# Linear attention feeding a PReLU MLP on one core: norm steps moved ahead of the evacuations, two PSUM banks for the output tiles, and tokens on partitions from batch 2 instead of batch 3

## The chip, the cores and the metric

The kernel runs on one core of one Trainium2 chip. The metric is the device time of that core in microseconds. An execution's time is a little longer than its span, which runs from the first to the last instruction of the trace.

## The reference

Eight batches of eight heads, 576 tokens and 64 features each go through attention without a softmax, a root-mean-square norm, and a two-layer MLP:

```python
# attention, per batch and head: q, k, v are 576 x 64
kv = einsum('bhsd,bhse->bhde', k, v)          # 64 x 64
out = einsum('bhsd,bhde->bhse', q, kv)
rms = sqrt(mean(out * out, axis=-1) + 1e-06)
x = (out / rms * g_norm)                       # -> 4608 tokens x 512
# MLP: 512 -> 2048 -> 512
h = x @ w_in
g = maximum(h, 0) + alpha * minimum(h, 0)
y = g @ w_out
```

Inputs and output are float32; the kernel multiplies in fp16 and accumulates in float32.

## The kernel before

**Tiling.** The 4608 tokens are cut into nine windows of 512 (`NW`, `W`), which do not coincide with the batches of 576. In a window the first layer makes 16 groups (`NF`) of 128 features: four matmuls of 512 columns into an `h_ps` bank (L422), then an evacuation on two engines: ScalarE writes `relu(-h)` to `m_sb` (L429) and VectorE writes `gt = beta * m_sb + h` (L431). The second layer makes four output tiles of 128 tokens by 512, each a sum of 16 matmuls (L444), copied out of PSUM by ScalarE (`y_sb`, L451) and stored by two transfers issued from SyncE (L459).

**Interleaving.** A unit (L530) is one group of the first layer for window w and four matmuls of the second layer for window w-1. In a steady window 16 units follow one another. PSUM has three banks for `h_ps`, one for `y_ps` (tag `y`), one shared bank (tag `s`) and three banks for attention (`o0`, `o1`, `o2`).

**Attention, first form** (windows below `NB_PE` = 3). For each pair of heads j: five transposes of q on TensorE (`step_t`, L207) and a copy by VectorE; the product k'v for all heads of a batch (`step_kv`, L222) and a masking multiply on VectorE; q times kv into `ot_ps` (`step_ot`), squared by ScalarE; a matmul with a block mask that sums the squares (`ssq_mm`, L270), then Ln and Exp on ScalarE; and the multiply `xt` on VectorE (`norm`, L281). The tail (L293 to L317) does the same for those tokens of the last such batch that reach into the next window: 192 tokens here, in two pieces.

**Attention, second form** (batches 3 to 7, "tokens on partitions"). q of a batch is transposed by one DMA (`transpose_q`, L328). For each tile of 128 tokens, four short matmuls write `otm_ps` and ScalarE squares it (`tile_a`, L336); VectorE reduces (`tile_b`, L349); ScalarE takes Ln and Exp of the small result, and GpSimd spreads the factor times g over the row, `rg` (`tile_c`, L357); VectorE multiplies, `xrow`, and SyncE issues DMA transposes into `xm`, the next window's input (`tile_d`, L370). `phase_steps(w)` (L383) lists these steps so that a tile's a, b and c, d fall in three successive units: b runs in the middle of a unit, behind the evacuation in VectorE's order; c, a and d at its end.

**Order.** Every engine's instructions run in the order written here; SyncE and GpSimd each have their own. GpSimd issues the loads of k, q, v and of the weights (casting to fp16), copies k and q of batches 2 to 7 into another layout (`regroup`, L105), and does `rg`. There are two sets of buffers for q, k and v, so batch b+2 overwrites batch b.

**Start.** Batch 0 arrives in halves and is handled in the first form; single matmuls on constants (`keep_warm`, L193) fill some gaps. Then come the 16 groups of window 0, the second layer of window 0 for three of its four tiles with window 1's attention between (L521), window 1's first layer with the fourth tile and window 2's attention between (L543), and from window 2 on the steady units (L561). At the end stands the second layer of window 8 alone.

Of the kernel before, what the change touches and what calls it, by code (L numbers as in the profile page):

```python
# [9 lines left out]
FP32 = mybir.dt.float32  # L10
# [7 lines left out]
def kernel(  # L18
# [11 lines left out]
    nc = tc.nc  # L30
# [15 lines left out]
    NC = D_MODEL // P  # L46
    assert NC == NPAIR and 0 < REM < P
    inv_d = 1.0 / D
    NB_PE = 3

    const_p = ctx.enter_context(tc.tile_pool(name="constp", bufs=1))
    w_p = ctx.enter_context(tc.tile_pool(name="weights", bufs=1))
# [56 lines left out]
        )  # L109

    def load_batch(b):
        for nm in ("k", "q", "v"):
            load(b, nm)

    def regroup_batch(b):
        for nm in ("k", "q"):
            regroup(b, nm, eng=nc.gpsimd)

    for nm in "qkv":
# [12 lines left out]
    nc.vector.memset(mask32[64:128, 64:128], 1.0)  # L132
    mask16 = const_p.tile([P, P], FP16, name="mask16")
    nc.vector.tensor_copy(out=mask16[:], in_=mask32[:])
    warm16 = const_p.tile([P, W], FP16, name="warm16")
    nc.vector.memset(warm16[:], 0.5)
    eps_t = const_p.tile([P, 1], FP32, name="eps_t")
# [8 lines left out]
    nc.sync.dma_start(out=g2col[64:128, :], in_=g_norm[:].unsqueeze(1))  # L146
    alpha_row = const_p.tile([NF, P], FP32, name="alpha_row")
    nc.sync.dma_start(out=alpha_row[:], in_=moe_alpha[:].rearrange("(g p) -> g p", p=P))
    g_all = const_p.tile([P, D], FP32, name="g_all")
    nc.sync.dma_start(out=g_all[:], in_=g_norm[:].partition_broadcast(P))  # L150


    WQ = 4
# [36 lines left out]
        load_w_out(i)  # L190


    def keep_warm(n):  # L193
        ps = ps_s.tile([P, W], FP32, name="warm_ps", tag="s")
# [71 lines left out]
    def step_ssq(w, j):  # L266
        ssq_mm(w, j)
        norm(w, j)

    def ssq_mm(w, j):  # L270
        ot_ps, sq = ots.pop((w, j))
        ssq_ps = ps_o.tile([P, W], FP32, name="ssq_ps", tag="o2")
        nc.tensor.matmul(out=ssq_ps[:], lhsT=mask16[:], rhs=sq[:], start=True, stop=True)  # L273
        rstd = attn_p.tile([P, W], FP32, name="rstd")
        nc.scalar.activation(  # L275
            out=rstd[:], in_=ssq_ps[:], func=AF.Ln, bias=eps_t[:], scale=inv_d,
        )
        nc.scalar.activation(out=rstd[:], in_=rstd[:], func=AF.Exp, bias=0.0, scale=-0.5)  # L278
        ots[w, j] = (ot_ps, rstd)

    def norm(w, j):  # L281
        ot_ps, rstd = ots.pop((w, j))
        xts[w, j] = xt_p.tile([P, W], FP16, name="xt", tag=f"xt{j}")
        nc.vector.scalar_tensor_tensor(  # L284
            out=xts[w, j][:], in0=ot_ps[:], scalar=g2col[:], in1=rstd[:],
            op0=ALU.mult, op1=ALU.mult,
        )
# [48 lines left out]
    def tile_a(b, t):  # L336
        ot_ps = ps_o.tile([P, H, D], FP32, name="otm_ps", tag=f"o{n_tile[0] % 3}")
        n_tile[0] += 1
        for j in range(NPAIR):
            nc.tensor.matmul(  # L340
                out=ot_ps[:, 2 * j : 2 * j + 2, :], lhsT=qtms[b][:, t * NPAIR + j, :],
                rhs=kvs[b, j], start=True, stop=True,
            )
        n = P if t < TPP else REM
        sq = attn_p.tile([P, H, D], FP32, name="sqm_sb", tag="rstd")
        nc.scalar.activation(out=sq[0:n], in_=ot_ps[0:n], func=AF.Square)  # L346
        tiles[b, t] = [n, ot_ps, sq]

    def tile_b(b, t):  # L349
        n, _, sq = tiles[b, t]  # L350
        ss = attn_p.tile([P, H], FP32, name="ss", bufs=3)
        nc.vector.tensor_reduce(  # L352
            out=ss[0:n], in_=sq[0:n], op=ALU.add, axis=mybir.AxisListType.X,
        )
        tiles[b, t][2] = ss

    def tile_c(b, t):  # L357
        n, _, ss = tiles[b, t]
        nc.scalar.activation(  # L359
            out=ss[0:n], in_=ss[0:n], func=AF.Ln, bias=eps_t[0:n], scale=inv_d,  # L360
        )
        nc.scalar.activation(out=ss[0:n], in_=ss[0:n], func=AF.Exp, bias=0.0, scale=-0.5)  # L362
        rg = attn_p.tile([P, H, D], FP32, name="rg")
        nc.gpsimd.tensor_tensor(  # L364
            out=rg[0:n], in0=ss[0:n].unsqueeze(2).to_broadcast([n, H, D]),
            in1=g_all[0:n].unsqueeze(1).to_broadcast([n, H, D]), op=ALU.mult,
        )
        tiles[b, t][2] = rg

    def tile_d(b, t):  # L370
        n, ot_ps, rg = tiles.pop((b, t))
        x = attn_p.tile([P, H, D], FP16, name="xrow", bufs=3)
        nc.vector.tensor_mul(out=x[0:n], in0=ot_ps[0:n], in1=rg[0:n])  # L373
        i = 0
        while i < n:
            w, c = divmod(b * S + t * P + i, W)
            m = min(n - i, W - c)
            nc.sync.dma_start_transpose(
                out=xm(w)[:, :, c : c + m], in_=x[i : i + m].rearrange("p h d -> p (h d)"),
            )  # L380
            i += m

    def phase_steps(w):  # L383


        if w >= NW:
            return []
        todo = [(b, t) for b in range(NB_PE, min(B, w + 1)) for t in range(NT)
                if (b, t) not in done and b * S + t * P < (w + 1) * W]
        done.update(todo)  # L390
        steps = []
        if w == NB_PE:
            n = NPAIR // JT
            for i in range(n + 1):
                m = [lambda i=i: step_tail_ot(i)] if i < n else []
                m += [lambda i=i: step_tail_ssq(i - 1)] if i > 0 else []
                steps.append(([], m))
        for i in range(len(todo) + 2):
            a, b, d = ([todo[i - k]] if 0 <= i - k < len(todo) else [] for k in range(3))
            mid = [lambda x=x: tile_b(*x) for x in b]  # L400
            end = [lambda x=x: tile_c(*x) for x in b] + [lambda x=x: tile_a(*x) for x in a]
            end += [lambda x=x: tile_d(*x) for x in d]
            steps.append((mid, end))
        if w < B:
            steps[0][0].append(lambda: step_kv(w))
        return steps

    done = set()
# [40 lines left out]
    def y_out(y, w, a):  # L449
        y_sb = ysb_p.tile([P, D_MODEL], FP32, name="y_sb")  # L450
        nc.scalar.copy(out=y_sb[:], in_=y[:])  # L451
        for i in range(0, P, REM):
# [5 lines left out]
                rows = out[b * S + LONG : (b + 1) * S, :].rearrange("(p t) m -> t p m", t=TPP)  # L458
            nc.sync.dma_start(out=rows[t], in_=y_sb[i : i + REM, :])  # L459


    H_POOL = (ps_h, "h")
    keep_warm(10)
# [1 line left out]
    step_t(0, 0, H_POOL)  # L465
    step_t(0, 1, H_POOL)
    regroup(0, "k", 0, HH)
    keep_warm(3)
    step_kv(0, 0, 2)
    step_ot(0, 0)  # L470
    step_ot(0, 1)
    regroup(0, "q", HH, H)
# [11 lines left out]
    )  # L484
    regroup(0, "k", HH, H)
    ssq_mm(0, 0)
    ssq_mm(0, 1)
    step_kv(0, 2, 4)
    norm(0, 0)
    norm(0, 1)  # L490
    step_ot(0, 2)
    step_ot(0, 3, (ps_y, "y"))
    load_batch(2)
    first = [ps_h.tile([P, W], FP32, name="h_ps", tag="h") for g in range(3)]
    for g in range(3):
        m1_mm(first[g], 0, g, (0, 1))
    step_ssq(0, 2)
    keep_warm(2)
    step_ssq(0, 3)
    for g in range(3):  # L500
        m1_mm(first[g], 0, g, (2,))
    for g in range(3):
        m1_mm(first[g], 0, g, (3,))
        m1_evac(first[g], 0, g)
    for g in range(3, NF):
        m1_group(0, g)
        if g == 10:
            regroup(1, "k")
        if g == 14:
            regroup(1, "q")  # L510

# [18 lines left out]
    def unit_m1_m2(w, g, y, mid):  # L530
        m1_group(w, g)
        mid()
        a, part = divmod(g, TPW)
        for gg in range(part * TPW, (part + 1) * TPW):
            y_mm(y, w - 1, a, gg)
        if part == TPW - 1:
            y_out(y, w - 1, a)


    steps = window_steps(2)  # L540
    n = len(steps)
    y = ps_y.tile([P, W], FP32, name="y_ps", tag="y")
    for g in range(NF):  # L543
        if g == 3:
            load_batch(3)
            regroup_batch(3)
        m1_group(1, g)
        if g > 3 and steps:
            steps.pop(0)()
        y_mm(y, 0, AHEAD, g)  # L550
        if g > 3 and steps:
            steps.pop(0)()
        if g == NF - 3:
            transpose_q(3)
    y_out(y, 0, AHEAD)

    LOAD_G = 6  # L560
    for w in range(2, NW):  # L561
        steps = phase_steps(w + 1)
        for g in range(NF):
            if g == LOAD_G and w + 2 < B:
                load_batch(w + 2)
            if g % TPW == 0:
                y = ps_y.tile([P, W], FP32, name="y_ps", tag="y")
# [43 lines left out]
```

## Time and profile before

| | us |
|---|---|
| median of 14 executions | 322.02 |
| lowest, highest of them | 320.18, 325.62 |
| the profiled execution: its time | 320.18 |
| the profiled execution: its span | 318.4 |

The profile names engines PE (TensorE matmul), PEld (TensorE weight load), DVE (VectorE), ACT (ScalarE), POOL (GpSimd) and SP (SyncE). A row of the timeline has the start, the duration, the engine, the source line, what is written from what with the shape, the count of merged instructions, and in brackets how long the engine had been idle and what released it. Matmuls are pipelined: a row's duration includes the run-out of the last matmul, so the time that a group takes is read from the start of one row to the start of the next. PEclk is the share of full clock that TensorE was granted.

### The profile page before, as it was taken

How to read it: one execution, taken by the hardware profiler on the slowest of the kernel's cores; microseconds unless marked ns; L12 is line 12 of the kernel's file. 1: busy time of each engine (PE TensorE's matmuls, PEld its weight loads, DVE VectorE, ACT ScalarE, POOL GpSimd, SP SyncE). 2: the span in 40 equal slices, each digit the busy share in tenths (PEclk: the TensorE clock that was granted, in tenths of full speed). 3: DMA queues.
4: the chain of work that ended last, by engine and by line, in shares of the span. 5: the costliest groups of instructions: out<-in, count | busy, mean ns of one | idle time of the engine just before them, and what ended most of it. 6: DMA issues, size and time to landing. Idle time of an engine off the chain costs nothing.

```text
span 318.4 us, 4199 instructions
## 1 busy us (share of the span) xinstructions
PE 287.9 (90%) x1526; PEld 135.9 (43%) x1526; DVE 162.4 (51%) x249; ACT 152.4 (48%) x298; POOL 96.7 (30%) x105
## 2 busy tenths in 40 slices
PE   5568999899997998999889989997899899999994
PEld 2223354444542453445334544453344444444441
DVE  4437933667555446644763457445734574443300
ACT  1355538388653445535454364436444644444211
POOL 8833309420028303650374236313200310000000
PEclk9979999999997999999999999999999999999999
DMA  6999999990119953795349826962331231111232
GB/s 79 189 206 202 202 202 134 225 170 2 33 34 152 187 115 60 98 218 124 66 57 209 183 49 84 213 149 50 44 82 33 51 74 33 35 33 33 56 79 66
DMA packets 61156, 34.33 MB, mean 108 GB/s; under 512 B 27840, under 2 KB 56528, under 8 KB 61136
## 3 DMA queue, kind: packets, MB, share of 16 engines
q0 software_dynamic: 29664, 18.35, 41.4%
q1 hardware_dynamic: 31472, 15.71, 22.8%
q8 instruction: 12, 0.20, 0.3%
q14 instruction: 8, 0.07, 0.1%
HBM read 36.74 MB, written 9.44 MB: 145 GB/s over the span
## 4 chain that ended last, share of the span: by engine, by line
PE 56%; ACT 15%; DMA 9%; DVE 8%; issue 6%; POOL 4%; ACTq 0%; DVEq 0%; POOLq 0%
PE h_ps L422 24%; PE y_ps L444 23%; DMA vst<-in_v_dram 7%; ACT m_sb L429 6%; DVE ss L352 4%; ACT sqm_sb L346 3%; PE kv_ps L232 3%; DVE gt L431 2%; ACT ss L359 2%; DMA qst<-in_q_dram 2%; ACT rstd L275 1%; ACT ss L362 1%; PE qt_ps L211 1%; PE ssq_ps L273 1%; POOL qst L96 1%
## 5 line engine op out<-in xcount | busy, mean ns | idle before, releaser
L431 DVE SCALAR_TENSOR_TENSOR gt<-m_sb,beta_sb,h_ps 128x512 f16<-128x512 f32 x144 | 106.6, 746 | 106.8 <-ACT m_sb L429 105.7
L444 PE MATMUL y_ps<-w_out_sb,gt 128*128 128x512 f16 x528 | 135.7, 381 | 5.3 <-ACT y_sb L451 5.3
L429 ACT ACTIVATE m_sb<-h_ps 128x512 f32<-128x512 f32 x144 | 84.7, 594 | 76.3 <-PE h_ps L422 76.1
L422 PE MATMUL h_ps<-xm,w_in_sb 128*128 128x512 f16 x384 | 98.5, 379 | 0.0
L444 PEld LDWEIGHTS <-gt 128*128 128x128 f16 x576 | 56.0, 98 | 73.2 <-issue 10.8
L422 PEld LDWEIGHTS <-w_in_sb 128*128 128x128 f16 x576 | 55.6, 99 | 67.1 <-issue 8.0
L364 POOL TENSOR_TENSOR rg<-ss,g_all 128x512 f32<-128x512 f32 (+1 forms) x25 | 26.1, 1044 | 109.4 <-ACT ss L362 109.4
L422 PE MATMUL h_ps<-xt,w_in_sb 128*128 128x512 f16 x192 | 49.7, 392 | 2.8 <-DVE xt L284 1.5
L451 ACT COPY y_sb<-y_ps 128x512 f32<-128x512 f32 x33 | 19.3, 584 | 16.7 <-PE y_ps L444 16.3
L359 ACT ACTIVATE ss<-ss,eps_t 128x8 f32<-128x8 f32 (+1 forms) x25 | 7.5, 301 | 34.2 <-DVE ss L352 34.2
L106 POOL COPY ksb<-kst 128x2560 f16<-128x2560 f16 x6 | 13.9, 2318 | 19.3 <-DMA kst<-in_k_dram 19.3
L346 ACT ACTIVATE sqm_sb<-otm_ps 128x512 f32<-128x512 f32 (+1 forms) x25 | 14.5, 582 | 8.0 <-PE otm_ps L340 8.0
L106 POOL COPY qsb<-qst 128x2560 f16<-128x2560 f16 x6 | 13.9, 2323 | 14.3 <-DMA qst<-in_q_dram 14.3
L373 DVE TENSOR_TENSOR xrow<-otm_ps,rg 128x512 f16<-128x512 f32 (+1 forms) x25 | 17.0, 678 | 2.1 <-POOL rg L364 2.1
L352 DVE TENSOR_REDUCE ss<-sqm_sb 128x8 f32<-128x512 f32 (+1 forms) x25 | 16.9, 677 | 0.0
L284 DVE SCALAR_TENSOR_TENSOR xt<-ot_ps,g2col,rstd 128x512 f16<-128x512 f32 x12 | 8.9, 749 | 13.5 <-ACT rstd L278 13.5
L263 ACT ACTIVATE sq_sb<-ot_ps 128x512 f16<-128x512 f32 x12 | 6.9, 589 | 17.1 <-PE ot_ps L257 17.1
L340 PE MATMUL otm_ps<-kv_sb,qtm 128*128 128x128 f16 x100 | 9.6, 218 | 5.4 <-DVE xrow L373 5.4
L232 PE MATMUL kv_ps<-vst,ksb 128*128 128x128 f16 x160 | 10.4, 219 | 4.3 <-DMA vst<-in_v_dram 2.8
L232 PEld LDWEIGHTS <-ksb 128*128 128x128 f16 x160 | 9.4, 98 | 8.4 <-issue 6.1
L340 PEld LDWEIGHTS <-qtm 128*128 128x128 f16 x100 | 7.7, 97 | 12.4 <-issue 7.3
L275 ACT ACTIVATE rstd<-ssq_ps,eps_t 128x512 f32<-128x512 f32 x12 | 8.2, 684 | 5.8 <-PE ssq_ps L273 5.8
(56 smaller groups left out, 132.4 us busy)
## 6 DMA issues: line engine op xcount, KB each, us to landing
out_dram<-y_sb SPq DMA_DIRECT2D x72, 128.0 KB, 2.4
kst<-in_k_dram POOLq DMA_DIRECT2D x7, 320.0 KB, 4.7
qst<-in_q_dram POOLq DMA_DIRECT2D x7, 320.0 KB, 8.8
vst<-in_v_dram POOLq DMA_DIRECT2D x7, 320.0 KB, 11.6
w_in_sb<-in_moe_w_in_dram POOLq DMA_DIRECT2D x4, 512.0 KB, 10.2
w_out_sb<-in_moe_w_out_dram POOLq DMA_DIRECT2D x4, 512.0 KB, 15.4
kst<-in_k_dram POOLq DMA_DIRECT2D x7, 256.0 KB, 6.3
qst<-in_q_dram POOLq DMA_DIRECT2D x7, 256.0 KB, 10.0
```

The lines of the kernel that those rows point to most:

```text
L106: (eng or nc.vector).tensor_copy(out=bufs[b % NBUF][nm][:, :, h0:h1, :].rearrange("p t h d -> p h t d"), in_=stages[b % NBUF][nm][:, h0:h1],)
L232: nc.tensor.matmul(out=kv_ps[:, j - j0, :], lhsT=ks(t), rhs=vs(t), start=(t == 0), stop=(t == NT - 1),)
L340: nc.tensor.matmul(out=ot_ps[:, 2 * j : 2 * j + 2, :], lhsT=qtms[b][:, t * NPAIR + j, :], rhs=kvs[b, j], start=True, stop=True,)
L346: nc.scalar.activation(out=sq[0:n], in_=ot_ps[0:n], func=AF.Square)
L352: nc.vector.tensor_reduce(out=ss[0:n], in_=sq[0:n], op=ALU.add, axis=mybir.AxisListType.X,)
L364: nc.gpsimd.tensor_tensor(out=rg[0:n], in0=ss[0:n].unsqueeze(2).to_broadcast([n, H, D]), in1=g_all[0:n].unsqueeze(1).to_broadcast([n, H, D ...
L373: nc.vector.tensor_mul(out=x[0:n], in0=ot_ps[0:n], in1=rg[0:n])
L422: nc.tensor.matmul(out=h_ps[:], lhsT=w_in_blk(c, g), rhs=xt_of(w, c), start=(c == 0), stop=(c == NC - 1),)
L429: nc.scalar.activation(out=m_sb[:], in_=h_ps[:], func=AF.Relu, scale=-1.0)
L431: nc.vector.scalar_tensor_tensor(out=gt[:], in0=m_sb[:], scalar=beta_sb[:, g : g + 1], in1=h_ps[:], op0=ALU.mult, op1=ALU.add,)
L444: nc.tensor.matmul(out=y[:], lhsT=gts[w, g][:, a * P : (a + 1) * P], rhs=w_out_blk(g), start=(g == 0), stop=(g == NF - 1),)
L451: nc.scalar.copy(out=y_sb[:], in_=y[:])
```

## The change

- `NB_PE` is 2: window 2 gets the second form, from batch 2 on. The tail is then 128 tokens of batch 1 in one piece. `phase_steps(2)` is spread over the units of window 1, which join the common loop (with one matmul of the fourth output tile in each unit).
- A step now has three places. At the beginning of a unit stand `tile_b` and `tile_d`, so that both stand ahead of the unit's evacuation in VectorE's order; in the middle `tile_c` (and `step_kv`), behind the group's evacuation; at the end `tile_a` and the tail.
- The output tiles of windows 1 to 7 alternate between the banks `y` and `s`.
- Loads of a batch go q, k, v instead of k, q, v. Batch 2's q and k are copied by VectorE in the second layer of window 0 (after groups 9 and 13), its q is transposed there by DMA, and the loads of batch 3 start there, behind a one-element GpSimd copy that waits for that transpose (`gate`).
- The broadcast of g over all partitions, a DMA at the start before, is made later by a matmul with ones (`spread_g`).
- At the start there are more `keep_warm` matmuls, `norm` of pairs 0 and 1 stands earlier, and pairs 2 and 3 use other banks, with the sums of squares between the first groups of the first layer.

```diff
-    NB_PE = 3
+    NB_PE = 2
...
-        for nm in ("k", "q", "v"):
+        for nm in ("q", "k", "v"):
             load(b, nm)
...
-        for nm in ("k", "q"):
+        for nm in ("q", "k"):
             regroup(b, nm, eng=nc.gpsimd)
...
-    g_all = const_p.tile([P, D], FP32, name="g_all")
-    nc.sync.dma_start(out=g_all[:], in_=g_norm[:].partition_broadcast(P))
...
-                steps.append(([], m))
+                steps.append(([], [], m))
         for i in range(len(todo) + 2):
             a, b, d = ([todo[i - k]] if 0 <= i - k < len(todo) else [] for k in range(3))
-            mid = [lambda x=x: tile_b(*x) for x in b]
-            end = [lambda x=x: tile_c(*x) for x in b] + [lambda x=x: tile_a(*x) for x in a]
-            end += [lambda x=x: tile_d(*x) for x in d]
-            steps.append((mid, end))
+            begin = [lambda x=x: tile_b(*x) for x in b] + [lambda x=x: tile_d(*x) for x in d]
+            mid = [lambda x=x: tile_c(*x) for x in b]
+            end = [lambda x=x: tile_a(*x) for x in a]
+            steps.append((begin, mid, end))
         if w < B:
-            steps[0][0].append(lambda: step_kv(w))
+            steps[0][1].append(lambda: step_kv(w))
...
+    def spread_g():
+        diag = const_p.tile([P, D], FP32, name="diag")
+        nc.vector.tensor_scalar(
+            out=diag[0:D], in0=ident[0:D, 0:D], scalar1=g2col[0:D], scalar2=None, op0=ALU.mult,
+        )
+        g_ps = ps_y.tile([P, D], FP32, name="g_ps", tag="y")
+        nc.tensor.matmul(
+            out=g_ps[:], lhsT=ones32[0:D], rhs=diag[0:D], start=True, stop=True,
+        )
+        nc.vector.tensor_copy(out=g_all[:], in_=g_ps[:])
...
-    keep_warm(3)
+    keep_warm(4)
     step_kv(0, 0, 2)
+    keep_warm(2)
     step_ot(0, 0)
...
     ssq_mm(0, 0)
+    keep_warm(3)
     ssq_mm(0, 1)
+    norm(0, 0)
+    keep_warm(3)
     step_kv(0, 2, 4)
-    norm(0, 0)
     norm(0, 1)
-    step_ot(0, 2)
+    step_ot(0, 2, (ps_o, "o2"))
     step_ot(0, 3, (ps_y, "y"))
     load_batch(2)
     first = [ps_h.tile([P, W], FP32, name="h_ps", tag="h") for g in range(3)]
-    for g in range(3):
+    m1_mm(first[0], 0, 0, (0, 1))
+    ssq_mm(0, 2, (ps_s, "s"))
+    for g in (1, 2):
         m1_mm(first[g], 0, g, (0, 1))
-    step_ssq(0, 2)
-    keep_warm(2)
-    step_ssq(0, 3)
+    ssq_mm(0, 3, (ps_o, "o0"))
+    keep_warm(6, (ps_o, "o1"))
+    norm(0, 2)
+    norm(0, 3)
     for g in range(3):
         m1_mm(first[g], 0, g, (2,))
+    keep_warm(2, (ps_o, "o1"))
...
+        if g == 12:
+            spread_g()
...
+        if g == 9:
+            regroup(2, "q")
+            transpose_q(2)
+        if g == 13:
+            gate = const_p.tile([1, 1], FP16, name="gate")
+            nc.gpsimd.tensor_copy(out=gate[:], in_=qtms[2][0:1, 0, 0:1])
+            load_batch(3)
+            regroup(2, "k")
     for a in range(AHEAD):
         y_out(ys[a], 0, a)
-    regroup_batch(2)
...
-    for w in range(2, NW):
+    for w in range(1, NW):
         steps = phase_steps(w + 1)
         for g in range(NF):
-            if g == LOAD_G and w + 2 < B:
+            if g == LOAD_G and 3 < w + 2 < B:
                 load_batch(w + 2)
-            if g % TPW == 0:
-                y = ps_y.tile([P, W], FP32, name="y_ps", tag="y")
-            mid, end = steps.pop(0) if steps else ([], [])
-            unit_m1_m2(w, g, y, lambda: [f() for f in mid])
+            a, part = divmod(g, TPW)
+            parts = range(part * TPW, (part + 1) * TPW)
+            if w == 1:
+                a, parts = AHEAD, [g]
+            begin, mid, end = steps.pop(0) if steps else ([], [], [])
+            for f in begin:
+                f()
+            m1_group(w, g)
+            for f in mid:
+                f()
+            if parts[0] == 0:
+                pool, tag = ((ps_y, "y"), (ps_s, "s"))[a % 2 if w > 1 else 0]
+                y = pool.tile([P, W], FP32, name="y_ps", tag=tag)
+            for gg in parts:
+                y_mm(y, w - 1, a, gg)
+            if parts[-1] == NF - 1:
+                y_out(y, w - 1, a)
             for f in end:
                 f()
```

The separate loops for window 1 (L540 to L555) and `unit_m1_m2` (L530) go.

More of the change, by code (lines that the diff above doesn't have):

```diff
@@ L134 @@
     nc.vector.tensor_copy(out=mask16[:], in_=mask32[:])
+    ones32 = const_p.tile([P, P], FP32, name="ones32")
+    nc.vector.memset(ones32[:], 1.0)
     warm16 = const_p.tile([P, W], FP16, name="warm16")
@@ L190, with keep_warm @@
         load_w_out(i)
-    def keep_warm(n):
-        ps = ps_s.tile([P, W], FP32, name="warm_ps", tag="s")
+    def keep_warm(n, pool=(ps_s, "s")):
+        ps = pool[0].tile([P, W], FP32, name="warm_ps", tag=pool[1])
         for i in range(n):
@@ L268, in step_ssq, with ssq_mm @@
         norm(w, j)
-    def ssq_mm(w, j):
+    def ssq_mm(w, j, pool=(ps_o, "o2")):
         ot_ps, sq = ots.pop((w, j))
-        ssq_ps = ps_o.tile([P, W], FP32, name="ssq_ps", tag="o2")
+        ssq_ps = pool[0].tile([P, W], FP32, name="ssq_ps", tag=pool[1])
         nc.tensor.matmul(out=ssq_ps[:], lhsT=mask16[:], rhs=sq[:], start=True, stop=True)
@@ L459, in y_out @@
             nc.sync.dma_start(out=rows[t], in_=y_sb[i : i + REM, :])
+    g_all = const_p.tile([P, D], FP32, name="g_all")
+    def spread_g():
[8 more added lines that the diff above has]
+        nc.vector.tensor_copy(out=g_all[:], in_=g_ps[:])
     H_POOL = (ps_h, "h")
@@ L525 @@
                 steps.pop(0)()
+        if g == 9:
[6 more added lines that the diff above has]
+            regroup(2, "k")
     for a in range(AHEAD):
         y_out(ys[a], 0, a)
-    regroup_batch(2)
[L530 to L541, printed above, removed]
-    y = ps_y.tile([P, W], FP32, name="y_ps", tag="y")
[L543 to L555, printed above, removed]
     LOAD_G = 6
-    for w in range(2, NW):
+    for w in range(1, NW):
         steps = phase_steps(w + 1)
         for g in range(NF):
-            if g == LOAD_G and w + 2 < B:
+            if g == LOAD_G and 3 < w + 2 < B:
                 load_batch(w + 2)
-            if g % TPW == 0:
-                y = ps_y.tile([P, W], FP32, name="y_ps", tag="y")
-            mid, end = steps.pop(0) if steps else ([], [])
-            unit_m1_m2(w, g, y, lambda: [f() for f in mid])
+            a, part = divmod(g, TPW)
[15 more added lines that the diff above has]
+                y_out(y, w - 1, a)
             for f in end:
```

## Prediction

> **What bounds the kernel now.** I read the page first for the span, then cut the trace into its stages (a boundary wherever a window's first `h_ps` matmul starts), then asked what TensorE waited for, and last went through one steady unit in the timeline.
>
> ```profile
> span 318.4 us, 4199 instructions
> ```
>
> The stages, from window 1 on (start:end, length, then each engine's busy time with instruction counts, TensorE's clock, DMA share, GB/s):
>
> ```profile
> 54.33:78.74 24.41, 22.09 (x133) 11.04 (x132) 16.33 (x25) 16.82 (x31) 7.50 (x7) 1.00 0.77 132
> 78.74:112.76 34.02, 31.92 (x168) 15.24 (x167) 17.43 (x27) 17.69 (x36) 11.86 (x11) 0.95 0.69 106
> 112.76:143.80 31.04, 29.96 (x166) 14.54 (x164) 17.14 (x26) 15.22 (x32) 12.88 (x12) 1.00 0.73 116
> 143.80:176.90 33.10, 30.50 (x170) 14.73 (x169) 18.34 (x28) 15.98 (x35) 13.90 (x13) 1.00 0.69 121
> 176.90:208.47 31.57, 30.12 (x166) 14.44 (x165) 17.23 (x26) 15.25 (x32) 12.87 (x13) 1.00 0.75 128
> 208.47:241.30 32.83, 29.79 (x165) 14.28 (x164) 18.39 (x27) 15.39 (x34) 5.25 (x6) 1.00 0.37 71
> 241.30:272.13 30.83, 29.71 (x150) 13.81 (x148) 16.57 (x25) 15.88 (x33) 4.17 (x4) 1.00 0.23 49
> 272.13:299.76 27.63, 27.63 (x130) 12.55 (x129) 11.96 (x17) 11.91 (x20) 0.00 (x0) 1.00 0.17 39
> ```
>
> The last row is window 8, which has no attention beside it: 16 units of eight matmuls in 27.63 us, 1.73 us a unit, 0.216 us a matmul, TensorE busy throughout. That is the floor of a unit. Windows 2 to 7 (the six rows above it) take 193.4 us. What attention itself adds on TensorE stands in window 3's first unit:
>
> ```profile
> 113.62 1.28 PE L232 MATMUL kv_ps<-vst,ksb 128*128 128x128 f16 x20
> 114.74 1.03 PE L444 MATMUL y_ps<-w_out_sb,gt 128*128 128x512 f16 x4
> 115.60 0.39 PE L340 MATMUL otm_ps<-kv_sb,qtm 128*128 128x128 f16 x4
> 115.82 0.38 PE L422 MATMUL h_ps<-xm,w_in_sb 128*128 128x512 f16 x1
> ```
>
> From start to start, a `step_kv` costs 1.12 us and a tile 0.22 us. After the change windows 2 to 7 hold five `step_kv` and 27 tiles (5, 4, 5, 4, 5, 4), so TensorE alone needs 6 x 27.63 + 5 x 1.12 + 27 x 0.22 = 177.3 us. That is 16.1 us less than the 193.4 of today, and the tile count hardly differs (25 there now, with a tail of two pieces beside them). So some 16 us are waiting. For what, the waits of TensorE over the whole span say (us in total, times, longest):
>
> ```profile
> PE otm_ps L340 <- DVE xrow L373: 5.4, 7, 0.9
> PE y_ps L444 <- ACT y_sb L451: 5.3, 8, 2.1
> ...
> PE kv_ps L232 <- DMA vst<-in_v_dram: 2.8, 3, 2.1
> ```
>
> The idle times start at the modelled end of the last matmul, so they show only part of what the stage lengths lose. The first two are one thing: banks that come free late because ScalarE and VectorE run behind. Here is why, in a unit of window 3, ScalarE first, then VectorE and GpSimd:
>
> ```profile
> 121.92 0.30 ACT L359 ACTIVATE ss<-ss,eps_t 64x8 f32<-64x8 f32 x1 [1.46 <-DVE ss L352]
> 122.25 0.21 ACT L362 ACTIVATE ss<-ss 64x8 f32<-64x8 f32 x1
> 122.37 0.57 ACT L346 ACTIVATE sqm_sb<-otm_ps 128x512 f32<-128x512 f32 x1
> 122.85 0.58 ACT L429 ACTIVATE m_sb<-h_ps 128x512 f32<-128x512 f32 x1
> 123.32 0.57 ACT L451 COPY y_sb<-y_ps 128x512 f32<-128x512 f32 x1
> 124.90 0.30 ACT L359 ACTIVATE ss<-ss,eps_t 128x8 f32<-128x8 f32 x1 [1.00 <-DVE ss L352]
> ```
>
> ```profile
> 123.46 0.75 DVE L431 SCALAR_TENSOR_TENSOR gt<-m_sb,beta_sb,h_ps 128x512 f16<-128x512 f32 x1 [1.03 <-ACT m_sb L429]
> 124.12 0.68 DVE L352 TENSOR_REDUCE ss<-sqm_sb 128x8 f32<-128x512 f32 x1
> 124.72 0.67 DVE L373 TENSOR_TENSOR xrow<-otm_ps,rg 64x512 f16<-64x512 f32 x1
> ```
>
> ```profile
> 122.54 1.03 POOL L364 TENSOR_TENSOR rg<-ss,g_all 64x512 f32<-64x512 f32 x1 [1.92 <-ACT ss L362]
> ```
>
> It is a ring: Ln waits for the reduce, the reduce stands behind `gt`, `gt` waits for the relu, and the relu stands behind the previous Ln, Exp and square. From one Ln to the next: 124.90 - 121.92 = 2.98 us, against 1.73 + 0.22 = 1.95 us of TensorE. Each tile unit loses about 1 us until the three `h_ps` banks and the one `y_ps` bank are used up; then TensorE pays.
>
> **The change, part by part. Steps at begin, middle, end.** The reduce now precedes `gt` and the relu precedes Ln, so the ring opens. What is left, by the durations just shown: VectorE has 0.68 + 0.67 + 0.75 = 2.10 us a unit; ScalarE 0.58 + 0.30 + 0.21 + 0.57 = 1.66. The path square, reduce, Ln, Exp, next square is 0.57 + 0.68 + 0.30 + 0.21 plus handovers, about 2.0. So VectorE sets 2.1, still 0.15 over TensorE, about 0.6 us over the four fullest units, and 0.57 where a `y_sb` copy goes before a square. New is that `xrow`, which waits for GpSimd, stands ahead of `gt`: Exp ends, `rg` takes 1.03, and `xrow` comes only after the next reduce, so I find it waiting 0.2 us at most. An `h_ps` bank is needed again three units (5.8 us) later, its `gt` ends about 3 us after the unit's start, so 2.9 us of cover stand against a lag of 1.3. I take nothing lost; bounds 0 and, without that cover, 1.1 us a window.
>
> **Two y banks.** The copy of an output tile has four units of cover instead of a few tenths of a us; 5.3 us of waits go. Bank `s` is shared with `step_kv` in the first unit of a window, but its copy is issued just before and has 0.86 us of `h_ps` matmuls to end in. Nothing is late there.
>
> **Loads.** They are issued on GpSimd behind the last `rg` of a window, and that now comes earlier. Of the 2.8 us of waits on v the longest, 2.1, is one; the other two make 0.7 that shows. I keep 1.0 for them, bounds 0 and 2. Another 0.5 is kept for the rest. So windows 2 to 7 take 177.3 + 1.5 = 178.8: **14.6 us less** than 193.4; bounds 10 and 16.1.
>
> **Clock.** Inside window 2's row the clock is 0.95. Its place:
>
> ```profile
> 98.12 1.02 PE L444 MATMUL y_ps<-w_out_sb,gt 128*128 128x512 f16 x4 [2.10 <-ACT y_sb L451]
> 98.98 1.55 PE L422 MATMUL h_ps<-xt,w_in_sb 128*128 128x512 f16 x4
> ```
>
> The four matmuls after 98.98 run near half rate, following a wait of 2.1 us. 0.05 x 34.02 = 1.7 us; it is inside the 16.1 and goes with the wait. The Trainium skill, "TensorE: Matmul & The Clock Gate" (Part 1), lets the clock fall only after an idle window of about 3.4 us; here 2.1 us was followed by it, so the trace goes against that rule as far as it is a length of idleness. By the rule no wait below would cost clock.
>
> **Window 2 in the second form, window 1's stage.** Gone from 54.33:78.74 are batch 2's 20 transposes, four `ot`, four `ssq`, eight long ScalarE steps, and four copies and four `norm` on VectorE. Come: `step_kv` 1.12 (as before), a tail of 0.22 + 0.22, three tiles 0.66. TensorE: 80 matmuls x 0.216 = 17.3, in all 19.5 us of 24.4. But two things bind first. *The loads of batch 2*: GpSimd's copies show when k and q were usable:
>
> ```profile
> 47.89 2.32 POOL L106 COPY ksb<-kst 128x2560 f16<-128x2560 f16 x1 [7.25 <-DMA kst<-in_k_dram]
> 50.84 2.32 POOL L106 COPY qsb<-qst 128x2560 f16<-128x2560 f16 x1 [0.63 <-DMA qst<-in_q_dram]
> ```
>
> 2.95 us a tensor, so v follows at 53.8; in the new order q 47.9, k 50.8, v 53.8. The DMA engines are full then, and the transpose of q is new work in the middle:
>
> ```profile
> 44.00:48.00 4.00, 4.00 (x28) 2.06 (x27) 1.18 (x3) 2.40 (x4) 0.11 (x1) 1.00 1.39 198
> 67.60:71.60 4.00, 3.45 (x21) 1.59 (x19) 3.19 (x5) 3.85 (x8) 0.00 (x0) 1.00 0.73 164
> ```
>
> A share of 1.39 under loads; batch 3's transpose alone (second row) makes 0.73 x 4.0 = 2.9, so 2.9 / 1.39 = 2.1 us at full rate. v lands at 55.9 (bounds 53.8, were it free, and 56.7). `step_kv(2)` stands in unit 0. TensorE cannot go past it, so the first unit ends no earlier, whatever the start saves. The Trainium skill, "DMA: Bandwidth & Descriptors" (SWDGE vs HWDGE vs iDMA), says that each DMA engine takes turns between the queues of both kinds, which speaks against this edit: by it the transpose takes up to its own 2.1 us from k and v. No row here shows turns taken.
>
> *VectorE*: `step_kv` at 55.9, then 1.12 + 0.22 + 0.22 + 1.08 + 0.22 puts unit 2 at 58.8. The tail's `norm` waits for a square sum, Ln and Exp and ends about 2.5 us after that (0.35 until ScalarE is free, and three steps like these:)
>
> ```profile
> L284 DVE SCALAR_TENSOR_TENSOR xt<-ot_ps,g2col,rstd 128x512 f16<-128x512 f32 x12 | 8.9, 749 | 13.5 <-ACT rstd L278 13.5
> ...
> L275 ACT ACTIVATE rstd<-ssq_ps,eps_t 128x512 f32<-128x512 f32 x12 | 8.2, 684 | 5.8 <-PE ssq_ps L273 5.8
> ```
>
> Then five `gt`, three reduces and three `xrow` follow, 5 x 0.75 + 6 x 0.68 = 7.8, with 0.7 of waiting for `rg`: 11.05 us after unit 2's start the `gt` of unit 6 ends, on which unit 9's bank hangs. TensorE would have been there after 8.2; 2.8 us are lost (bounds 0 and 4). Seven more units of 1.08: window 2 starts at 58.8 + 11.05 + 7.6 = 77.4 instead of 78.74, **1.3 us less**; bounds 6 less (no waits, v early) and 2 more (one window at half clock besides).
>
> **Start.**
>
> ```profile
> 18.21 2.76 PE L422 MATMUL h_ps<-xt,w_in_sb 128*128 128x512 f16 x6
> ...
> 24.65 0.81 PE L422 MATMUL h_ps<-xt,w_in_sb 128*128 128x512 f16 x3 [0.43 <-DVE xt L284]
> ```
>
> Six matmuls at half rate (0.43 each) stand ahead of the square sum of pair 2; only two will, so `xt` comes 4 x 0.43 = 1.7 us sooner, about 2 with full clock from the added `keep_warm`. These fill waits; if they do not, the 15 added cost 15 x 0.216 = 3.2. But v at 55.9 takes the 2 us back: TensorE would reach `step_kv` at 53.2 and wait. Net nothing on the sum. The broadcast of g and the `gate` are off the path: `rg` needs g and GpSimd first in unit 3.
>
> **Sum.** 320.18 - 14.6 - 1.3 = 304.3 for an execution like the profiled one. That was the fastest of its 14, 1.84 under their median 322.02. The forecast for the median is 304.3 + 1.8 = **306**.
>
> **The rivals.** *A, the start slips* (15%): v comes later still, the wait of 2.7 us before `step_kv` draws half clock as at 98.98 (1.7) and VectorE lags 1 more: 309. For it, that row; against it, 2.7 us spread over two clock windows may not suffice. *B, VectorE binds in the steady units* (10%): each tile unit keeps 0.15 to 0.2, 27 x 0.2 = 5.4: 311. Against it, the 2.9 us of cover. *C, no late v* (9%): the start's 2 us and part of VectorE's lag are kept: 302. *D, slower* (4%): `xrow` ahead of `gt` makes VectorE wait for GpSimd in every tile unit. One serial round is square, reduce, Ln, Exp, `rg`, `xrow`, `gt`: 0.57 + 0.68 + 0.51 + 1.03 + 0.67 + 0.75 = 4.2 us. 27 x (4.2 - 1.95) = 61, less six windows' cover of 2.9, is 43 over the forecast: 349. It ends slower from about 3.2 us a round, (16.1 + 17.4) / 27 above 1.95. For it, GpSimd is idle 1.9 us for want of Exp in its row; against it, nothing in the round needs the same unit's `gt`. *E, no gain* (2%): DMA, not the ring, frees the banks.
>
> **Numbers.** The forecast, 303.5 to 308, has 60%. The range 301 to 312 takes in A, B and C. About 0.3%, 1 us, is what a measurement of this kernel can tell from no change: faster 0.94, within it 0.02 (E), slower 0.04 (D).
>
> **What would show it.** Right: windows 2 to 7 of 29 to 30.3 us each, no wait on `xrow` or `y_sb` in TensorE's list, clock 1.00 in window 2; `kv_ps` waiting 2 to 3 us for v near 53 to 56; `h_ps` waiting for `gt` in window 1's units 7 to 9. Wrong: windows still above 31, VectorE idle before `xrow` for `rg`, or window 2 starting after 80.

## The result, and the profile after

| | us |
|---|---|
| before, median of 48 executions | 322.03 (318.62 to 325.62) |
| after, median of 10 | 302.9 (301.52 to 303.53) |
| ratio after / before | 0.9409, 95% interval 0.9384 to 0.9433 |
| the profiled execution after: time, span | 303.14, 301.2 |

Medians of the experiments below are over all executions of a run (4, 6 or 10); ratios and their intervals leave out the slow ones, such as one execution of experiment 6 with 383.1 us at a granted clock of 0.755.

The stages of the kernel after, cut as before at the first `h_ps` matmul of windows 1 to 8 (same columns):

```profile
54.60:77.39 22.79, 20.15 (x118) 9.82 (x117) 17.07 (x25) 14.45 (x31) 11.93 (x12) 1.00 1.14 175
77.39:107.25 29.86, 29.86 (x169) 14.75 (x168) 18.85 (x29) 17.30 (x36) 13.93 (x13) 1.00 0.76 128
107.25:136.88 29.63, 29.63 (x165) 14.52 (x164) 17.39 (x26) 15.83 (x32) 12.88 (x12) 1.00 0.88 138
136.88:166.74 29.86, 29.86 (x169) 14.77 (x168) 18.55 (x28) 16.84 (x35) 13.92 (x13) 1.00 0.79 126
166.74:196.39 29.65, 29.65 (x166) 14.52 (x165) 17.42 (x26) 15.85 (x32) 12.88 (x12) 1.00 0.89 149
196.39:226.24 29.85, 29.85 (x169) 14.76 (x168) 18.52 (x28) 16.84 (x35) 5.21 (x5) 1.00 0.26 56
226.24:254.75 28.51, 28.51 (x145) 13.42 (x144) 16.79 (x25) 15.85 (x32) 4.17 (x4) 1.00 0.24 53
```

In the last six rows TensorE's busy time equals the length of the stage. Windows 2 to 7 take 254.75 - 77.39 = 177.4 us; TensorE's own work had been put at 177.3. Before they took 193.4. A tile unit of window 3, ScalarE and then VectorE:

```profile
111.93 0.30 ACT L359 ACTIVATE ss<-ss,eps_t 128x8 f32<-128x8 f32 x1
112.26 0.21 ACT L362 ACTIVATE ss<-ss 128x8 f32<-128x8 f32 x1
112.47 0.59 ACT L346 ACTIVATE sqm_sb<-otm_ps 64x512 f32<-64x512 f32 x1
113.33 0.60 ACT L429 ACTIVATE m_sb<-h_ps 128x512 f32<-128x512 f32 x1 [0.27 <-PE h_ps L422]
113.87 0.30 ACT L359 ACTIVATE ss<-ss,eps_t 64x8 f32<-64x8 f32 x1
```

```profile
113.09 0.68 DVE L352 TENSOR_REDUCE ss<-sqm_sb 64x8 f32<-64x512 f32 x1 [0.33 <-ACT sqm_sb L346]
113.69 0.67 DVE L373 TENSOR_TENSOR xrow<-otm_ps,rg 128x512 f16<-128x512 f32 x1
114.29 0.73 DVE L431 SCALAR_TENSOR_TENSOR gt<-m_sb,beta_sb,h_ps 128x512 f16<-128x512 f32 x1
```

From one Ln to the next it is 113.87 - 111.93 = 1.94 us, where it was 2.98. The relu now waits for TensorE (0.27, `h_ps`), and no longer stands behind a Ln that waits for a reduce. What TensorE still waits for, longest first:

```profile
PE warm_ps L196 <- DVE eps_t L140: 3.3, 1, 3.3
PE h_ps L422 <- DVE gt L431: 2.1, 3, 1.0
PE g_ps L470 <- DVE diag L466: 2.0, 1, 2.0
PE otm_ps L340 <- DVE xm L314: 1.2, 1, 1.2
PE kv_ps L232 <- DMA vst<-in_v_dram: 0.7, 1, 0.7
```

`xrow` and `y_sb` are gone from the list. Everything left lies in the first 70 us. New, and not foreseen, is `g_ps`, the matmul that spreads g. VectorE and TensorE around it:

```profile
31.96 0.84 DVE L106 COPY ksb<-kst 128x2560 f16<-128x2560 f16 x1
32.73 1.39 DVE L431 SCALAR_TENSOR_TENSOR gt<-m_sb,beta_sb,h_ps 128x512 f16<-128x512 f32 x2
34.04 0.24 DVE L466 TENSOR_SCALAR diag<-ident,g2col 64x64 f32<-64x64 f32 x1
```

```profile
34.33 0.43 PE L470 MATMUL g_ps<-diag,ones 64*128 64x64 f32 x2 [1.97 <-DVE diag L466]
34.70 4.45 PE L422 MATMUL h_ps<-xt,w_in_sb 128*128 128x512 f16 x12
38.98 0.38 PE L444 MATMUL ya<-w_out_sb,gt 128*128 128x512 f16 x1
```

`diag` stands behind the copy of batch 1's k and the evacuations of groups 11 and 12 in VectorE's order; the matmul stands right behind group 12 on TensorE. VectorE works without a gap from the copy to `diag`, and TensorE waits for the end of it. The 12 matmuls after it take 4.28 us (34.70 to 38.98), where 40 before it took 8.79, because the clock fell:

```profile
23.57:32.36 8.79, 8.79 (x40) 3.81 (x39) 7.55 (x11) 5.51 (x10) 3.63 (x5) 1.00 1.35 201
35.37:38.78 3.41, 3.41 (x10) 1.21 (x9) 1.19 (x2) 1.19 (x2) 1.35 (x2) 0.50 1.25 206
```

3.41 us at half rate cost 1.7 us, and the executions fall into two groups that fit it: those with a mean clock of 0.999 or 1.000 took 301.5 to 302.2 us, those with 0.990 to 0.994 took 302.6 to 303.5.

### The profile page after: what moved, and what is told of

Same layout as the page of the kernel before. It is cut to its first block, busy times and chain, and to the rows that moved or that the text cites. A ratio compares the mean times of both kernels' runs of the same rounds, so it can differ in the third digit from the quotient of the medians.

```text
span 301.2 us, 4238 instructions
## 1 busy us (share of the span) xinstructions
PE 284.8 (95%) x1530; PEld 136.6 (45%) x1530; DVE 166.7 (55%) x255; ACT 153.1 (51%) x298; POOL 97.7 (32%) x109
## 4 chain that ended last, share of the span: by engine, by line
PE 86%; POOL 3%; DMA 3%; ACT 3%; DVE 2%; issue 2%; POOLq 0%; ACTq 0%
PE h_ps L422 39%; PE y_ps L444 37%; PE kv_ps L232 3%; DMA w_in_sb<-in_moe_w_in_dram 3%; PE otm_ps L340 2%; DVE gt L431 1%; PE ya L444 1%; PE yb L444 1%; PE yc L444 1%; ACT m_sb L429 1%; PE warm_ps L196 1%; PE ssq_ps L273 1%; DVE ksb L106 1%; POOL qst L96 0%; ACT rstd L275 0%
## 5 line engine op out<-in xcount | busy, mean ns | idle before, releaser
L422 PE MATMUL h_ps<-xm,w_in_sb 128*128 128x512 f16 x448 | 115.0, 379 | 0.0
L444 PEld LDWEIGHTS <-gt 128*128 128x128 f16 x576 | 55.9, 98 | 65.7 <-issue 1.2
L364 POOL TENSOR_TENSOR rg<-ss,g_all 128x512 f32<-128x512 f32 (+1 forms) x30 | 31.3, 1042 | 86.5 <-ACT ss L362 85.7
L422 PE MATMUL h_ps<-xt,w_in_sb 128*128 128x512 f16 x128 | 32.9, 395 | 2.2 <-DVE gt L431 2.1
L352 DVE TENSOR_REDUCE ss<-sqm_sb 128x8 f32<-128x512 f32 (+1 forms) x30 | 20.5, 683 | 9.6 <-ACT sqm_sb L346 9.5
L346 ACT ACTIVATE sqm_sb<-otm_ps 128x512 f32<-128x512 f32 (+1 forms) x30 | 17.8, 592 | 9.3 <-PE otm_ps L340 9.3
L373 DVE TENSOR_TENSOR xrow<-otm_ps,rg 128x512 f16<-128x512 f32 (+1 forms) x30 | 20.4, 681 | 3.6 <-POOL rg L364 3.6
L106 POOL COPY qsb<-qst 128x2560 f16<-128x2560 f16 x5 | 11.6, 2317 | 11.6 <-issue 8.9
L196 PE MATMUL warm_ps<-warm,mask 128*128 128x512 f16 x30 | 9.7, 462 | 3.8 <-DVE eps_t L140 3.3
L263 ACT ACTIVATE sq_sb<-ot_ps 128x512 f16<-128x512 f32 x8 | 4.5, 589 | 15.6 <-PE ot_ps L257 15.6
L284 DVE SCALAR_TENSOR_TENSOR xt<-ot_ps,g2col,rstd 128x512 f16<-128x512 f32 x8 | 6.0, 749 | 9.0 <-ACT rstd L278 9.0
```

The costliest lines, as they stand in the source:

```text
L106: (eng or nc.vector).tensor_copy(out=bufs[b % NBUF][nm][:, :, h0:h1, :].rearrange("p t h d -> p h t d"), in_=stages[b % NBUF][nm][:, h0:h1],)
L352: nc.vector.tensor_reduce(out=ss[0:n], in_=sq[0:n], op=ALU.add, axis=mybir.AxisListType.X,)
L364: nc.gpsimd.tensor_tensor(out=rg[0:n], in0=ss[0:n].unsqueeze(2).to_broadcast([n, H, D]), in1=g_all[0:n].unsqueeze(1).to_broadcast([n, H, D ...
L422: nc.tensor.matmul(out=h_ps[:], lhsT=w_in_blk(c, g), rhs=xt_of(w, c), start=(c == 0), stop=(c == NC - 1),)
L444: nc.tensor.matmul(out=y[:], lhsT=gts[w, g][:, a * P : (a + 1) * P], rhs=w_out_blk(g), start=(g == 0), stop=(g == NF - 1),)
```

## The experiments

The theory was that the ring relu, `gt`, reduce, Ln made the waits, and that putting the reduce first opened it. The rival was that the second y bank did it; TensorE's list of waits before had given the two 5.4 and 5.3 us. Ratios are to the kernel before.

**1. The old places of the norm steps.**

```diff
-            begin = [lambda x=x: tile_b(*x) for x in b] + [lambda x=x: tile_d(*x) for x in d]
-            mid = [lambda x=x: tile_c(*x) for x in b]
-            end = [lambda x=x: tile_a(*x) for x in a]
+            begin = []
+            mid = [lambda x=x: tile_b(*x) for x in b]
+            end = [lambda x=x: tile_c(*x) for x in b] + [lambda x=x: tile_a(*x) for x in a]
+            end += [lambda x=x: tile_d(*x) for x in d]
```

> The changed kernel with the norm steps put back where they stood (reduce in the middle of the unit, Ln, Exp and the row factor, the next tile and the multiply at its end); the two y banks and all else stay. Ring theory (the waits come from the ring relu - Ln - reduce - gt, 2.98 us a tile unit): windows 2 to 7 lose 8 to 12 us again against the changed kernel's 302.9, so 311 to 315, and TensorE waits for xrow. Rival, bank theory (the single y bank was what made TensorE wait): the second bank is still there, so at most 3 us are lost, under 306.

Measured: 323.8 us, ratio 1.0062 (1.0019 to 1.0104). With the old places the rest of the change gains nothing; it is even a little slower than the kernel before. The loss is 20.9 us, twice the 8 to 12 expected. In its profile (326.57 us) windows 2 to 7 take 195.1 us (83.02 to 278.16) instead of 177.4 and window 1 takes 28.2 (from 54.82) instead of 22.8. So the greater part of the miss is that windows 2 to 7 lose all that the new places had won there; the rest is window 1, which has tiles too now, beside units of 1.1 us of TensorE. TensorE's first three waits:

```profile
PE otm_ps L340 <- DVE xrow L373: 7.8, 9, 0.9
PE kv_ps L232 <- DMA vst<-in_v_dram: 5.6, 4, 2.8
PE h_ps L423 <- DVE gt L432: 4.4, 4, 1.7
```

The waits for v are part of it: GpSimd issues a window's loads behind its last row factor, and with the ring that comes late.

**2. One y bank.**

```diff
-                pool, tag = ((ps_y, "y"), (ps_s, "s"))[a % 2 if w > 1 else 0]
+                pool, tag = ((ps_y, "y"), (ps_s, "s"))[0]
```

> The changed kernel with all output tiles in one bank; the new places of the norm steps stay. Ring theory: the copy of an output tile comes late only in the one or two tile units of a window in which a tile ends, by some 0.5 us, so 1 to 3 us are lost, 304 to 306. Bank theory: most of the 16 us come back, over 310.

Measured: 303.3 us, 0.9406 (0.9342 to 0.9470): no loss, and `y_sb` is not among TensorE's waits at all. The bank theory falls.

**3. Both undone.**

> The changed kernel with both undone, old places and one y bank: windows 2 to 7 should be as long as in the kernel before (193 us against 178), so 315 to 319. If the two edits are independent, the loss is the sum of the two single losses; by the ring theory it is a little more than the loss by the old places alone.

Measured: 324.5 us, 1.0076 (1.0037 to 1.0114), above the expected range and the same as experiment 1. The second bank is worth nothing that shows with the ring closed either: TensorE then waits 4.4 us for `y_sb` instead, inside the same total.

**4. The new places alone, in the kernel before.** The same lines, the other way.

> The kernel before with one edit of the change alone: reduce and multiply at the beginning of a unit, Ln, Exp and the row factor in its middle, the next tile at its end. One y bank, first form up to window 2, the old start. Order theory (the place of the norm steps is nearly all of the gain): windows 2 to 7 fall from 193 to 178 us, so 306 to 309. Rival (the other edits carry part of it, above all window 2 in the second form): 314 or more.

Measured: 308.6 us, 0.9603 (0.9494 to 0.9712). Some 13 of the 19 us come from where the reduce, Ln and multiply stand (9 to 16 by the interval; single executions took 304.9 to 311.2). In its profile, the fastest of the four, windows 2 to 7 take 178.6 us (78.20 to 256.79), and TensorE waits there neither for `xrow` nor for `y_sb`: the ring opens with one y bank and without the rest of the change.

**5 and 6. Which of the two moves.** The multiply back at the end:

```diff
-            begin = [lambda x=x: tile_b(*x) for x in b] + [lambda x=x: tile_d(*x) for x in d]
+            begin = [lambda x=x: tile_b(*x) for x in b]
...
-            end = [lambda x=x: tile_a(*x) for x in a]
+            end = [lambda x=x: tile_a(*x) for x in a] + [lambda x=x: tile_d(*x) for x in d]
```

> The changed kernel with the multiply (xrow) put back at the end of the unit, the reduce left at its beginning. Theory that the ring is closed by the reduce behind the evacuation: it stays open, 302 to 305. Rival (the late multiply, by holding its PSUM bank, is what stalls): 308 or more.

Measured: 302.3 us, 0.9422 (0.9325 to 0.9519), as the theory has it. Where the multiply stands makes no difference that shows, once the reduce is first. And the reduce back in the middle:

```diff
-            begin = [lambda x=x: tile_b(*x) for x in b] + [lambda x=x: tile_d(*x) for x in d]
-            mid = [lambda x=x: tile_c(*x) for x in b]
+            begin = [lambda x=x: tile_d(*x) for x in d]
+            mid = [lambda x=x: tile_b(*x) for x in b] + [lambda x=x: tile_c(*x) for x in b]
```

> The changed kernel with the reduce put back behind the evacuation, in the middle of the unit just ahead of Ln and Exp, the multiply left at the beginning. Ring theory: relu, evacuation, reduce, Ln, Exp, square and the next relu follow one another again, 0.6 + 0.75 + 0.68 + 0.3 + 0.2 + 0.57 = 3.1 us a tile unit, so most of the 21 us that the old order cost come back, 318 to 324. Rival (multiply is what matters): 303 to 306.

Measured: 345.5 us, 1.0795 (1.0733 to 1.0857), over 20 us worse than expected. VectorE there:

```profile
92.68 0.69 DVE L373 TENSOR_TENSOR xrow<-otm_ps,rg 128x512 f16<-128x512 f32 x1 [1.79 <-POOL rg L364]
93.29 0.74 DVE L431 SCALAR_TENSOR_TENSOR gt<-m_sb,beta_sb,h_ps 128x512 f16<-128x512 f32 x1
93.94 0.67 DVE L352 TENSOR_REDUCE ss<-sqm_sb 64x8 f32<-64x512 f32 x1
96.39 0.68 DVE L373 TENSOR_TENSOR xrow<-otm_ps,rg 64x512 f16<-64x512 f32 x1 [1.78 <-POOL rg L364]
97.00 0.73 DVE L431 SCALAR_TENSOR_TENSOR gt<-m_sb,beta_sb,h_ps 128x512 f16<-128x512 f32 x1
```

`gt` to `gt` 3.7 us. This is another ring than the one I named: multiply, `gt`, reduce, Ln, Exp, row factor, next multiply, with GpSimd in it. It is in the main the prediction's rival D, whose round had the square in it too, and it sits one edit away from the changed kernel: a multiply ahead of the evacuation is harmless only with the reduce ahead of it too.

**7. The diagonal of g early.** `diag` is made ahead of the copy of k's second half instead of in `spread_g`.

```diff
+    make_diag()
     regroup(0, "k", HH, H)
     ssq_mm(0, 0)
```

> The changed kernel with the one VectorE instruction that makes the diagonal of g issued before the second half of batch 0's k is copied, so that the matmul that spreads g no longer waits behind the evacuation of group 12. The wait of 2.0 us before it and the half clock after it should go, and the second layer of window 0 starts at about 35.3 instead of 39.0. Theory of the prediction (batch 2's loads then bind at step_kv of batch 2): only 0.5 to 2.5 us of the 3.7 arrive at the end, 300.4 to 302.4, with TensorE waiting at kv_ps. Rival (nothing binds there): all 3.7 arrive, 299.2.

Measured: 300.8 us, 0.9345 (0.9275 to 0.9415). The wait and the half clock are gone:

```profile
32.20 0.43 PE L471 MATMUL g_ps<-diag,ones 64*128 64x64 f32 x2
32.57 2.88 PE L422 MATMUL h_ps<-xt,w_in_sb 128*128 128x512 f16 x12
35.29 0.38 PE L444 MATMUL ya<-w_out_sb,gt 128*128 128x512 f16 x1
```

Of 38.98 - 35.29 = 3.7 us, 2.5 reach `step_kv` of batch 2 (53.47, against 55.99), which waits 0.95 for v.

**8. The old start** in the changed kernel, with the DMA that broadcasts g.

> The changed kernel with the start of the kernel before: the order of the first window's attention, its few warming matmuls and the DMA that broadcasts g at the start. If the new start gains nothing (its 2.9 us are lost again to the wait for the diagonal of g and the half clock behind it), 302 to 303.5. Rival (the new start is worth the 2 us that the prediction gave it): 304.5 to 306.

Measured: 306.2 us, 0.9527 (0.9475 to 0.9578). My theory of nothing gained fell; the new start is worth 3.3 us even with the wait for `diag` in it. The stages of this start:

```profile
0.00:10.96 10.96, 5.80 (x23) 2.16 (x23) 5.00 (x18) 1.28 (x1) 8.25 (x18) 1.00 0.84 107
10.96:24.61 13.65, 10.58 (x47) 5.48 (x48) 4.08 (x9) 5.59 (x10) 7.87 (x11) 0.50 1.28 201
24.61:40.71 16.10, 13.32 (x60) 5.68 (x59) 12.29 (x18) 10.48 (x18) 6.04 (x8) 1.00 1.33 202
```

Thirteen microseconds at half clock, four times 3.41, and the second layer begins at 40.71. In the profile of the kernel after the clock is 1.00 up to 35.37. So the new start keeps the clock up, and that is probably a large part of what it gains; whether the added warming matmuls do it, the new order or the missing DMA, this run doesn't tell, since it undoes all three. The kernel before has nearly the same start and fell to half there for one stretch of 3.4 us in its profile; why here for four stays open.

**9. Batch 3's loads not held back** (with the early diagonal).

```diff
-            nc.gpsimd.tensor_copy(out=gate[:], in_=qtms[2][0:1, 0, 0:1])
+            nc.gpsimd.tensor_copy(out=gate[:], in_=ident16[0:1, 0:1])
```

> The early diagonal, and the one-element copy of the gate reads a constant instead of the transposed q, so that batch 3's loads are queued at once, beside batch 2's transpose. Theory from the trace of the early diagonal (a transpose moves nothing while loads stand in GpSimd's queue): the transpose of batch 2 lands only when batch 3's loads are through, 7 to 9 us later than 56, TensorE waits for the first tile of batch 2, and the time is 304 to 309. Rival (the engines take turns between the two queues, as the prediction had it): it lands within 2 to 4 us of 56, and the time is 300 to 302.

Measured: 308.4 us, 0.9606 (0.9554 to 0.9658), 7.6 over experiment 7 and inside the expected range. The transpose, issued at 48.4, landed 16.3 us later, and TensorE's longest wait is

```profile
PE otm_ps L340 <- DMA qtm<-qsb: 7.2, 1, 7.2
```

But the theory's reason fell: the transpose does not stand still until the loads are through. It moves nothing until 52.3, 3.9 us after its issue, and from then on the two queues take turns. From 62 to 63 (queue: packets, MB, share of 16 engines):

```profile
q0 software_dynamic: 223, 0.13, 88.0%
q1 hardware_dynamic: 221, 0.06, 41.8%
```

`q0` is GpSimd's queue with the loads, `q1` holds the transpose. The rival had the turns right and their cost far too low; that the theory's range was met is luck.

**10, 11 and 12. Window 1 made looser**, all with the early diagonal. First batch 2's tiles in every other unit, `step_kv` one unit later, and the first tile in a bank that doesn't wait for the tail:

```diff
-    n_tile = [0]
+    n_tile = [1]
...
+        if w == NB_PE:
+            slots = [x for t in todo for x in (t, None)]
+        else:
+            slots = todo
...
-            steps[0][1].append(lambda: step_kv(w))
+            steps[1 if w == NB_PE else 0][1].append(lambda: step_kv(w))
```

> The changed kernel with the diagonal of g made early, step_kv of batch 2 one unit later in window 1, batch 2's three tiles in every other unit of window 1 and their banks starting at the second (so that the first does not wait for the tail's multiply). If window 1 lost its time to step_kv's wait for v (1.0) and to VectorE being filled by three successive tile units (2 to 3), 2.5 to 3.5 us go beside the 2.1 of the early diagonal: 297 to 298.5. Rival (VectorE's total in window 1 binds, however it is spread): no better than 300.8, the early diagonal alone.

Measured: 301.7 us, 0.9428 (0.9373 to 0.9483); a miss. Without the next tile's reduce before it, the multiply waits for the row factor ahead of `gt`, the GpSimd ring again:

```profile
62.21 0.69 DVE L373 TENSOR_TENSOR xrow<-otm_ps,rg 128x512 f16<-128x512 f32 x1 [2.07 <-POOL rg L364]
...
65.88 0.69 DVE L373 TENSOR_TENSOR xrow<-otm_ps,rg 128x512 f16<-128x512 f32 x1 [1.07 <-POOL rg L364]
...
69.55 0.69 DVE L373 TENSOR_TENSOR xrow<-otm_ps,rg 128x512 f16<-128x512 f32 x1 [1.08 <-POOL rg L364]
```

So the multiply one unit later, `step_kv` in unit 2 and the tiles from unit 3:

```diff
+        slots, late = todo, 2
+        if w == NB_PE:
+            steps.append(([], [], []))
+            slots, late = [x for t in todo for x in (t, None)], 3
...
-            steps[0][1].append(lambda: step_kv(w))
+            steps[2 if w == NB_PE else 0][1].append(lambda: step_kv(w))
```

> The early diagonal, batch 2's step_kv in unit 2 of window 1, its tiles from unit 3 on in every other unit, and the multiply three units behind its tile instead of two, so that a reduce always stands before it and the row factor has a unit more. If what spoiled the first spread was the multiply waiting for the row factor ahead of the evacuation (1.1 to 2.1 us three times), that is gone, window 1 takes 19.5 to 20.5 us and the time is 296.5 to 298. Rival (VectorE's total binds): 300 or more.

Measured: 299.2 us, 0.9317 (0.9268 to 0.9366), the lowest median here, 3.7 us under the changed kernel, though not the 298 expected; its interval overlaps those of experiments 7 and 12. Window 1's TensorE work ends at 71.9 now (51.68 to 71.89, 20.2 us), but window 2 waits for its input:

```profile
73.91 1.02 PE L428 MATMUL h_ps<-xm,w_in_sb 128*128 128x512 f16 x4 [1.86 <-DMA xm<-xrow]
```

The first of the three transposes of `xrow`, issued at 63.30 beside batch 3's loads, landed 9.3 us later; the others took 7.5 and 6.1. Hence the last try: v of batch 3 loaded in unit 9.

```diff
-            load_batch(3)
+            load(3, "q")
+            load(3, "k")
...
+            if w == 1 and g == LOAD_G + 3:
+                load(3, "v")
```

> The kernel with the early diagonal and the late spread, and batch 3's v loaded only in unit 9 of window 1, so that window 2's inputs are transposed while GpSimd's queue is empty. If those transposes were late because they stood behind batch 3's loads (the first landed 9.3 us after its issue, and window 2 began 1.9 us late), that wait goes and the time is 296.5 to 298.0. Rival (the transposes are late because SyncE issues them late): no change, 299 to 300.

Measured: 301.3 us, 0.9353 (0.9312 to 0.9394); a miss. The first two transposes landed sooner, after 4.4 and 4.2 us, as the theory has it, but v's load was issued at 66.8, just ahead of the third, which then took 7.4 us:

```profile
74.95 1.02 PE L428 MATMUL h_ps<-xm,w_in_sb 128*128 128x512 f16 x4 [3.15 <-DMA xm<-xrow]
```

## Why the prediction was right or wrong

**The ring: right.** Forecast 14.6 us less in windows 2 to 7, measured 16.0. The term that was off is the 1.5 us kept for v and the rest: nothing of it was needed. In window 3 v's load is issued 15.2 us after the window's start (at 122.48), where it was 19.5 (at 132.21), and no wait is left.

**The second bank: wrong, though the sum doesn't hang on it.** "5.3 us of waits go" was written under it. The waits went, but experiments 2, 3 and 4 show that the places of the steps took them. The prediction had said itself that the first two rows of the list are one thing, and then still gave the bank its row. The sum takes all the waiting of windows 2 to 7 out at once, so the time did not suffer.

**The multiply ahead of the evacuation: right, and close to the edge.** VectorE waits 3.6 us in all for the row factor in the kernel after, 0.5 at the longest where 0.2 at most had been written, and TensorE waits for none of it in windows 2 to 7. Experiments 6 and 10 show the price when the reduce isn't there to cover it.

**Window 1: the right number for the wrong reason.** Forecast: `step_kv` of batch 2 at 55.9, window 2 at 77.4. Measured:

```profile
54.60 1.04 PE L422 MATMUL h_ps<-xt,w_in_sb 128*128 128x512 f16 x4
55.99 1.29 PE L232 MATMUL kv_ps<-vst,ksb 128*128 128x128 f16 x20 [0.36 <-DVE ksb L106]
```

and 77.39. But v was not late: its load, issued at 39.4, landed 14.0 us later, at 53.4, so the 2.1 us for the transpose were wrong. Transposes and loads do take turns, as experiment 9 shows, but this transpose, issued at 51.37, moved its first packets only after 52, when v was nearly through. And TensorE was not early: it reached this place at 55.5, not 53.2. The failed step is "the broadcast of g and the `gate` are off the path". I looked only at who needs g, not at what the matmul that makes it waits for. Its 2.0 us and the half clock behind it ate the start's gain (pair 3's `xt` was used at 21.72 instead of 24.65, 2.9 us sooner), so that the two errors met. Experiment 7 separates them: with the wait gone, `step_kv` starts at 53.47, bound by v. That the start's gain would be partly taken back there was right; it was 1.2 us of 3.7, not all.

**VectorE in window 1: right in size, though one wait was another.** From unit 2's first matmul to unit 9's, 11.05 us were forecast; they are 58.85 to 69.84, 10.99. Of TensorE's waits in it 1.2 us is one that I had not named: the first tile's bank is the one that the tail's multiply frees. The waits that I had named, for `gt` at units 8 and 9, are 0.5 and 0.6.

**The median: wrong.** The 1.8 us by which the profiled execution lay under its median were carried over. The kernel after varies less (2.0 us from lowest to highest in 10 executions, against 7.0 in 48), and its profiled execution lies 0.2 above the median. Of the 3.1 us between 306 and 302.9 this makes 2.0. The rest is the 1.2 us between 304.3 and the profiled 303.14, mostly the 1.4 of windows 2 to 7.

## What to carry to other kernels

When two engines evacuate in turn and each also does a chain of small steps, write down one unit in both engines' orders and follow it round: a step that feeds the other engine belongs ahead of the step that waits for it. A wait list names the bank that runs out last, not the reason, and a one-off matmul is as dear as the queue in front of its operand. Before putting a cross-engine multiply first, ask what fills the engine while its operand is made. Where a DMA transpose is on the path, hold bulk loads back until it has landed: here that was worth 7.6 us.

## What the runs showed of the hardware

**A DMA transpose beside GpSimd's loads starts late, and then the two queues take turns packet by packet.** In experiment 7 the transpose of q was issued at 48.25 and landed 7.8 us later. From 48 to 51 the DMA traffic was

```profile
q0 software_dynamic: 1063, 0.59, 139.9%
```

GpSimd's queue alone; the transpose's queue has no row. In experiment 9 this silence lasts 3.9 us, against 1.2 in the kernel before, where a transpose issued at 67.62 has hardly a load beside it. After it the packets go one for one: 223 and 221 in the microsecond shown under experiment 9, where the loads without the transpose moved 373 (experiment 7, 48 to 49) and the transpose without loads 1135 (kernel before, 70 to 71). So both lose, and the transpose, which has the smaller packets (0.06 MB against 0.13 for the same number), is slowed most. With few loads beside them transposes of q land after 4.1 us (the median of the kernel before); beside one more batch of loads it was 16.3 (experiment 9). The Trainium skill, "DMA: Bandwidth & Descriptors" (SWDGE vs HWDGE vs iDMA), has the engines take turns between the two kinds of queue; the trace of experiment 9 agrees, once the transpose has begun. Why it begins so late beside loads, no run tells.

**Half clock comes in stretches of 3.41 us and after waits shorter than that.** The stretches are 35.37 to 38.78 in the kernel after and four times that length in experiment 8. A wait of 2.0 us was enough in the kernel after, with TensorE busy for 1.44 of the 3.41 us before the fall (31.96 to 35.37); and not always, as experiment 2's profile has the same wait of 2.0 and a clock of 0.999. The Trainium skill, "TensorE: Matmul & The Clock Gate" (Part 1), gives the window's length, 3413 ns, and lets it run freely against the kernel, which fits the two groups of times; that only an idle window of that length makes the clock fall does not fit.
